# Warm-up matmuls on a constant: 26 of 48 columns in place of six of 512, at the head of a gated attention and feed-forward kernel

## The chip, the cores and the metric

The kernel runs on one core of a Trainium2 chip. The metric is the device time of one execution in microseconds (us); lower is better. The core has a matrix engine (PE, whose weight loads are recorded apart as PEld), a vector engine (DVE), a scalar engine (ACT), a general engine (POOL), and a queue engine (SP) that here only issues DMA transfers.

## The reference

One input x of 2048 tokens by 640 features feeds two branches, and a gate for each token mixes them.

```python
def _A_ref(x, wqkv, w_phi, wo):                      # 32 heads of 20
    q, k, v = split(x @ wqkv)
    pq = einsum("bhsd,hdf->bhsf", q, w_phi); pk = einsum("bhsd,hdf->bhsf", k, w_phi)
    phi_q = concat([softmax(pq), softmax(-pq)]); phi_k = concat([softmax(pk), softmax(-pk)])
    kv = einsum("bhsf,bhsd->bhfd", phi_k, v);  z = sum(phi_k, over s)
    o = einsum("bhqf,bhfd->bhqd", phi_q, kv) / (einsum("bhqf,bhf->bhq", phi_q, z) + 1e-6)
    return o @ wo
def _B_ref(x, w_gate, w_up, w_down):                 # F = 1728
    return (gelu(x @ w_gate) * (x @ w_up)) @ w_down
g = sigmoid((x * gate_w).sum(-1))
return g * _A_ref(x, ...) + (1 - g) * _B_ref(x, ...)
```

## The kernel before

Tokens are taken in 16 tiles of 128. Features lie on the 128 partitions in five chunks (`kt`), so a product of one token tile with a weight is five accumulating matmuls. The order of the work on each engine is written out by hand: each call of `sc.op` appends one instruction to one engine's program, with the semaphore waits that its reads and writes need. Between two instructions of PE no wait is put in. An engine works through its program strictly in that order.

The run has two stages. `attention_state` builds the transposed input `xT`, folds `w_phi` into the query and key weights (`fold`, L374), projects v, k and q for each token tile (`mm`, L396) and sums the attention state (`gram`, L506). `ffn` then does the gate and up projections in blocks of 512 tokens (`gateup`, again L396) and the down projections with the output projection (`down_pair`, L717), with the attention numerators (`num`, L662) in between.

The change touches the first instructions of PE. `attention_state` begins with matmuls whose two operands are a constant of ones (L543 to L545): each has a 128 by 128 stationary block and a moving block of `n` columns, and each writes to bank 0 of the accumulator `ps`, where the next thing written overwrites it. Nothing reads what they compute. The steps behind them, in PE's order, are these:

- `x_transpose(0)` and `x_transpose(1)` (L331): for each, ten PE transposes of 64 by 64 blocks. They need `xtok`, tokens that a DMA loads (L225, two transfers), and the identity that POOL makes. DVE and ACT copy the results to `xT` (L341, L339).
- six more matmuls on the constant (L551, 64 rows, 128 columns), then `x_transpose(2)` and `(3)`, which need the second `xtok` transfer.
- `v_step` (L408): for each of five chunks and four tiles, one matmul of 480 and one of 160 columns. They need `xT` and the weight chunk `w` (L245, five transfers).
- `gate_column` (L356), then `v_tile(4)` and `(5)` (L396), three folds (L374), and so on. `v_tile(6)` is the first that needs `xT` of tiles 6 and 7.

`xT` of the tiles from 4 on comes by transposing DMAs (L233), as do the transposed weights `wkT` and `wqT` (L229). SP issues all of these one after another: `xtok` twice, five chunks of `w`, `xT` of tiles 4 and 5, `wkT`, `xT` of tiles 6 and 7, `wqT`, and the rest of `xT`. None of them waits for PE.

Of the kernel before, what the change touches and what calls it, by code (L numbers as in the profile page):

```python
# [107 lines left out]
class _Kernel:  # L108
# [430 lines left out]
    def attention_state(self):  # L539
        NT = self.NT  # L540
        sc = self.sc
        ones = self.nc.const_aps.tensor(1.0, [P, 512], BF16)
        for n in (512, 512, 512, 512, 512, 512, 128, 128, 128):  # L543
            sc.op("pe", lambda e: e.matmul(self.bank(0, n), ones[:, 0:P], ones[:, 0:n], start=True, stop=True),
                  writes=[("ps", 0)])  # L545
        vs, ve, xt = self.v_step, self.v_first_evac, self.x_transpose
        xt(0, "d")
        xt(1, "a")
        for i in range(3):
            for a, b in ((0, 2), (64, 3)):  # L550
                sc.op("pe", lambda e: e.matmul(self.bank(b, P), ones[a:a + 64, 0:P], ones[a:a + 64, 0:P], start=True,  # L551
                                               stop=True), writes=[("ps", b)])
        xt(2, "d")
        xt(3, "a")
        for kt in range(4):
            for t in range(4):
                vs(t, kt)
        self.blockdiag()
        self.gate_column(6)
        for t in range(4):  # L560
            vs(t, 4)
            ve([t], "ad"[t % 2], False)
            if t == 2:
                ve([0, 1, 2], "a", True)
        ve([3], "d", True)
        f, v, k, q = self.fold, self.v_tile, self.k_tile, self.q_tile
        v(4, 6)
        v(5, 0)
        f(0, "k", (2, 3))
        f(1, "k", (4, 5))  # L570
        f(2, "k", (6, 7))
        self.strip(6)
        f(3, "k", (0, 1))
        self.strip(0)
        v(6, 2)
        f(4, "k", (4, 5))
        v(7, 6)
        k(0, 0)
        f(0, "q", (2, 3))
        f(1, "q", (4, 5))  # L580
        k(1, 6)
        f(2, "q", (2, 3))
        self.k_sums(0)
        k(2, 0)
        f(3, "q", (2, 3))
        self.strip(2)
        f(4, "q", (4, 5))
        self.k_scale(0)
        k(3, 6)
        v(8, 0)  # L590
        for t in range(1, 4):
            self.k_norm(t)
        nk, nv, ng = 4, 9, 0
        pieces = self.gate_pieces()
        for s in range(NT):
            r = s % 4
            if r != 1:
                k(nk, 2)
                self.k_norm(nk)
                nk += 1  # L600
            if s and r != 0:
                self.gram(ng)
                ng += 1
            if s and r in (0, 1):
                v(nv, 0)
                nv += 1
            q(s, 6)
            if s:
                pieces.pop(0)()
        for p in pieces:  # L610
            p()
        self.down_weights()
# [240 lines left out]
```

## Time and profile before

| | |
|---|---|
| median of 3 runs | 284.88 us |
| lowest, highest | 284.87, 287.49 us |
| the profiled execution | 284.86 us |
| span of the profile, first to last instruction | 283.5 us |
| around the span | 284.86 - 283.5 = 1.36 us |
| PE busy, matmuls | 280.3 us of the span, 2922 matmuls |
| DVE, ACT, POOL busy | 172.8, 104.8, 13.2 us |
| DMA moved | 24.11 MB |
| granted clock, mean of the run | 1.000 |

Times in the profile count from the start of the span. "Idle" is the time that an engine stood still before an instruction, with what ended it. Matmuls are pipelined: a matmul's record lasts from its start to a modelled end, so records overlap and a busy PE need not stream at its best rate. The spacing between the starts of successive matmuls, or of their weight loads, is the better measure of pace. PEq stands for PE's sequencer and SPq for SP's issuing of DMAs; "issue" marks time in which an engine waited for nothing that the profile shows.

### The profile page before, as it was taken

The numbers are of one execution on the slowest core, as the hardware profiler recorded it, in microseconds if no ns is written. First come the engines' busy times: TensorE is split into PE (matmuls) and PEld (weight loads), VectorE is DVE, ScalarE is ACT, GpSimd is POOL, SyncE is SP. The second block draws the span as 40 slices with busy tenths as digits, with TensorE's granted clock in tenths as the row PEclk, the third lists the DMA queues.
The fourth block names the chain that finished last, engine by engine and source line by source line (L and its number), as shares of the span: only waits on it lengthen the run. The fifth ranks groups of instructions, "written<-read, shape, count | busy, mean of one in ns | idle before, by whom it ended". The sixth has DMA issues, their size and how long they took to land.

```text
span 283.5 us, 6887 instructions
## 1 busy us (share of the span) xinstructions
PE 280.3 (99%) x2922; PEld 174.7 (62%) x2922; DVE 172.8 (61%) x325; ACT 104.8 (37%) x191; POOL 13.2 (5%) x67
## 2 busy tenths in 40 slices
PE   8999999999999999999999999999999999999996
PEld 5677777777754444444444444445777777777786
DVE  1369999999995332667242334325883883884801
ACT  4357888887852223222332223231112112012011
POOL 7500101110000000000000000000000000000000
DMA  8994398989999500011000000000133233232221
GB/s 227 189 219 91 60 198 179 192 180 165 171 250 353 146 0 0 2 23 24 2 0 0 0 2 0 0 0 2 25 50 85 58 44 76 72 44 76 73 73 49
DMA packets 58922, 24.11 MB, mean 85 GB/s; under 512 B 50954, under 2 KB 58378, under 8 KB 58890
## 3 DMA queue, kind: packets, MB, share of 16 engines
q1 hardware_dynamic: 58224, 23.63, 38.8%
q8 instruction: 23, 0.38, 0.6%
q10 hardware_dynamic: 666, 0.03, 0.2%
q14 instruction: 9, 0.07, 0.1%
HBM read 9.04 MB, written 2.62 MB: 41 GB/s over the span
## 4 chain that ended last, share of the span: by engine, by line
PE 94%; SPq 3%; DMA 2%; issue 0%; ACT 0%
PE ps L396 61%; PE ps L717 28%; PE ps L662 2%; DMA xT<-in_A_x_dram 2%; PE ps L506 2%; SPq L229 1%; SPq L245 1%; PE ps L374 1%; SPq L233 1%; SPq L225 0%; ACT outsb L730 0%
## 5 line engine op out<-in xcount | busy, mean ns | idle before, releaser
L396 PE MATMUL ps<-xT,wu_sb 128*128 128x512 bf16 x260 | 64.6, 379 | 0.0
L396 PE MATMUL ps<-xT,wg_sb 128*128 128x512 bf16 x260 | 64.6, 379 | 0.0
L633 ACT ACTIVATE gl<-ps 128x512 bf16<-128x512 f32 x52 | 31.1, 598 | 76.0 <-PE ps L396 73.8
L635 DVE TENSOR_TENSOR hT<-ps,gl 128x512 bf16<-128x512 f32 x39 | 26.7, 691 | 43.2 <-PE ps L396 43.2
L717 PE MATMUL ps<-wd_sb,hT 64*128 64x320 bf16 x648 | 48.4, 296 | 0.0
L396 PEld LDWEIGHTS ps<-xT,wu_sb 128*128 128x128 bf16 x260 | 25.4, 98 | 30.9 <-DVE hT L635 0.4
L396 PEld LDWEIGHTS ps<-xT,wg_sb 128*128 128x128 bf16 x260 | 25.0, 98 | 29.4
L730 ACT ACTIVATE outsb<-ps,Gm 128x320 bf16<-128x320 f32 (+2 forms) x31 | 14.6, 516 | 71.7 <-PE ps L717 71.7
L396 PE MATMUL ps<-w,xT 128*128 128x304 bf16 (+3 forms) x280 | 40.6, 296 | 0.3 <-DMA xT<-in_A_x_dram 0.3
L717 PEld LDWEIGHTS ps<-wd_sb,hT 64*128 64x128 bf16 x648 | 30.9, 94 | 12.2 <-issue 0.4
L396 PEld LDWEIGHTS ps<-w,xT 128*128 128x128 bf16 x280 | 26.4, 97 | 10.2 <-DMA xT<-in_A_x_dram 0.5
L717 PE MATMUL ps<-wo_sb,goT 64*128 64x320 bf16 (+2 forms) x340 | 26.5, 288 | 0.0
L495 DVE TENSOR_TENSOR Ek<-Ek,Dk 128x1320 bf16<-128x1320 bf16 x16 | 24.5, 1532 | 0.5
L688 DVE TENSOR_TENSOR O<-ps,RH 128x640 bf16<-128x640 f32 x32 | 24.8, 817 | 0.0
L486 DVE TENSOR_REDUCE Dk<-Ek 128x66 f32<-128x1320 bf16 x16 | 24.3, 1520 | 0.0
L396 PE MATMUL ps<-wq,xT 128*128 128x304 bf16 x160 | 23.3, 292 | 0.0
L453 ACT ACTIVATE Eqt<-ps 128x627 bf16<-128x627 f32 x32 | 20.5, 694 | 6.5 <-PE ps L396 6.5
L453 ACT ACTIVATE Ek<-ps 128x627 bf16<-128x627 f32 x32 | 20.5, 694 | 2.8 <-PE ps L396 2.6
L635 DVE TENSOR_TENSOR xT<-ps,gl 128x512 bf16<-128x512 f32 x13 | 9.0, 692 | 18.2 <-PE ps L396 18.2
L717 PEld LDWEIGHTS ps<-wo_sb,goT 64*128 64x128 bf16 x340 | 15.9, 94 | 5.3
L396 PEld LDWEIGHTS ps<-wq,xT 128*128 128x128 bf16 x160 | 15.0, 98 | 4.5
L717 PE MATMUL ps<-wd_sb,xT 64*128 64x320 bf16 (+2 forms) x270 | 16.0, 269 | 0.0
(77 smaller groups left out, 180.1 us busy)
## 6 DMA issues: line engine op xcount, KB each, us to landing
out_dram<-outsb SPq DMA_DIRECT2D x7, 320.0 KB, 2.3
wd_sb<-in_B_w_down_dram SPq DMA_DIRECT2D x1, 2080.0 KB, 10.6
wg_sb<-in_B_w_gate_dram SPq DMA_DIRECT2D x5, 224.0 KB, 4.0
wu_sb<-in_B_w_up_dram SPq DMA_DIRECT2D x5, 224.0 KB, 3.4
wg_sb<-in_B_w_gate_dram SPq DMA_DIRECT2D x5, 192.0 KB, 3.7
wu_sb<-in_B_w_up_dram SPq DMA_DIRECT2D x5, 192.0 KB, 3.3
w<-in_A_wqkv_dram SPq DMA_DIRECT2D x5, 160.0 KB, 4.0
wo_sb<-in_A_wo_dram SPq DMA_DIRECT2D x1, 800.0 KB, 9.6
```

The lines of the kernel that those rows point to most:

```text
L229: sc.dma("sp", lambda e: e.dma_start_transpose(T[:, :, :], self.wqkv[:, c0:c0 + D]), writes=[key])
L396: self.sc.op("pe", lambda e: e.matmul(self.ps[:, bank * 512 + c0:bank * 512 + c0 + n], lhs, rhs, start=first, stop=fin), reads=reads, writ ...
L453: self.sc.op("act", lambda e: e.activation(dst, src, AF.Exp, scale=scale), reads=[("ps", b), ("ps", b + 1)], writes=[(name, sl, s)])
L486: self.sc.op("dve", lambda e: e.tensor_reduce(self.Dk[:, se, 0, :].rearrange("p (u h) -> p u h", h=self.HG), self.k_view(se), AX.X, ALU.ad ...
L495: sc.op("dve", lambda e: e.tensor_tensor(v, v, R.rearrange("p (u h) -> p u h", h=self.HG).unsqueeze(3).to_broadcast([P, 2 * self.G, self.H ...
L506: self.sc.op("pe", lambda e: e.matmul(self.bank(b)[:, c:c + n], self.Ek[:, se, g * P:(g + 1) * P], va[:, w * g:w * g + n], start=(t == 0 a ...
L633: sc.op("act", lambda e: e.activation(self.gl[:, slot, :], self.bank(banks[0]), AF.Gelu_apprx_tanh), reads=[("ps", banks[0])], writes=[("g ...
L635: sc.op("dve", lambda e: e.tensor_tensor(hT, self.bank(banks[1]), self.gl[:, slot, :], ALU.mult), reads=[("ps", banks[1]), ("gl", slot)], ...
L662: sc.op("pe", lambda e: e.matmul(self.ps[:, o:o + n], self.Eq[a:a + 64, g, t * P:(t + 1) * P], self.KV[a:a + 64, g, 0:n], start=(g in (0, ...
L688: dve(lambda e, o=o, f=f, s=s: e.tensor_tensor(o, V[s][:, :, 0:DH], f, ALU.mult), rb + [key(6 + s)], [("O", s, sl)], guard=old)
L717: sc.op("pe", lambda e: e.matmul(self.bank(bk, w), lhs, rhs, start=opens and x == 0, stop=end and not opens, skip_group_check=True), reads ...
L730: sc.op("act", lambda e: e.activation(dst, self.bank(bk, w), AF.Copy, scale=g), reads=rd, writes=wr)
```

## The change

The list of column counts of the constant matmuls is replaced. Before, there are six of 512 columns and three of 128; after, 26 of 48 columns and the same three of 128.

```diff
         ones = self.nc.const_aps.tensor(1.0, [P, 512], BF16)
-        for n in (512, 512, 512, 512, 512, 512, 128, 128, 128):
+        for n in [48] * 26 + [128] * 3:
             sc.op("pe", lambda e: e.matmul(self.bank(0, n), ones[:, 0:P], ones[:, 0:n], start=True, stop=True),
                   writes=[("ps", 0)])
```

The columns streamed by this loop go from 6 x 512 + 3 x 128 = 3456 to 26 x 48 + 3 x 128 = 1632, and its matmuls, each with a weight load, from 9 to 29. All else in the program stays as it is and where it is.

## The prediction

> **What bounds the kernel now.** I read the busy times of the page first, then what PE waited for over the whole run, then the chain of waits that ends at 30 us, and last the first 6 us of PE instruction by instruction.
>
> ```profile
> PE 280.3 (99%) x2922; PEld 174.7 (62%) x2922; DVE 172.8 (61%) x325; ACT 104.8 (37%) x191; POOL 13.2 (5%) x67
> ```
> ```profile
> PE ps L544 <- PEq L838: 0.8, 1, 0.8
> PE ps L396 <- DMA xT<-in_A_x_dram: 0.3, 1, 0.3
> ```
>
> The second fence is the whole answer for PE as the waiting engine. After its start at 0.84 us, PE stands still once in the run, for 0.3 us, and a DMA ends that. From there to the end PE alone sets the time, so whatever delays it past that wait is paid in full at the end. What paces the part ahead of it is in the chain that leads into that wait:
>
> ```profile
> 4.09 1.93 SPq L233
> 6.02 0.05 issue
> 6.07 3.70 SPq L229
> 9.77 0.04 issue
> 9.81 5.65 DMA xT<-in_A_x_dram
> 15.46 0.05 issue
> 15.51 1.54 PE ps L396 x10
> ```
>
> The columns are start, length and what. SP's issues follow one another and end in the transposing DMA for tiles 6 and 7, which lands at 15.46 us. Nothing of PE stands in this chain. Ahead of 15.5 us PE therefore has a slack, and these two rows give its size (the number in brackets is the idle time before the row):
>
> ```profile
> 15.51 0.76 PE L396 MATMUL ps<-w,xT 128*128 128x345 bf16 x4 [0.27 <-DMA xT<-in_A_x_dram]
> ```
> ```profile
> 15.51 0.56 PEld L396 LDWEIGHTS ps<-w,xT 128*128 128x128 bf16 x5 [0.46 <-DMA xT<-in_A_x_dram]
> ```
>
> The slack is 0.27 us by the matmul's modelled end and 0.46 us by the weight load. Matmul records overlap (the 512-column ones last 0.63 us and start 0.43 us apart), so a modelled end understates the idle time, and I take a value near the upper one, 0.40 us.
>
> Now the start, first as PE's weight loads in order of time:
>
> ```profile
> 1.22 0.15 PEld L544 LDWEIGHTS ps<-const-bfloat16-1.0 128*128 128x128 bf16 x1 [0.27 <-issue]
> 1.65 0.15 PEld L544 LDWEIGHTS ps<-const-bfloat16-1.0 128*128 128x128 bf16 x1 [0.28 <-issue]
> 2.07 0.15 PEld L544 LDWEIGHTS ps<-const-bfloat16-1.0 128*128 128x128 bf16 x1 [0.28 <-issue]
> ...
> 3.35 0.25 PEld L544 LDWEIGHTS ps<-const-bfloat16-1.0 128*128 128x128 bf16 x2 [0.28 <-issue]
> 3.80 0.19 PEld L331 LDWEIGHTS ps<-ident,xtok 64*128 64x128 bf16 x6 [0.20 <-DMA xtok<-in_A_x_dram]
> ```
>
> Two things are to be seen. The 512-column matmuls start 0.43 us apart, while a window of 5 us in the gate and up stage (100 to 105 us) holds 25 of the same width, some 0.21 us each: PE starts at half its later pace. And the transposes at 3.80 us are released by the landing of `xtok`, not by the end of the warm-up. Where the pace doubles shows in the groups of two stretches, 4 to 6 us and 6 to 9 us, where the last number is the mean record in ns:
>
> ```profile
> L408 PE MATMUL ps<-w,xT 128*128 128x480 bf16 x2 | 0.8, 456 | 0.0
> ```
> ```profile
> L408 PE MATMUL ps<-w,xT 128*128 128x480 bf16 x12 | 3.4, 364 | 0.0
> ```
>
> Two matmuls of 480 columns start between 4 and 6 us, at a mean of 456 ns; from 6 us on each takes 364. So one of the two took 2 x 456 - 364 = 548 ns, and that is the first (it starts at 5.31). The pace changes inside it: I put the change at 5.7 us, which is 5.7 - 0.84 = 4.86 us after PE's first matmul. The granted clock of the profile reads 1.00 in every stretch, so this doubling has to be read from the pace. PE was kept at work nearly without a break over those 4.86 us.
>
> **The warm-up itself.** Removed are six matmuls of 0.43 us (the first 0.38), from 0.84 to 3.35 us: 2.51 us. Added are 26 of 48 columns with 26 weight loads. At the slow pace 512 columns take 0.43 us, so 48 take 0.040 us, together 1.04 us. The nearest row for such short matmuls with a full weight load each is `gram`: 11 matmuls of 63 columns in 0.34 us of the chain at 29.52 us, 0.031 us each at the fast pace, so at most 0.062 us if everything in it is halved, together 1.61 us. I take the lower one, because the three 128-column matmuls in the same loop are paced by their columns (the load of 0.15 us lies beside them). With the three at 0.107 us (0.32 us), which stay, the loop ends at 2.2 us, at the latest at 2.8. On the path this is worth nothing: the transposes still wait for `xtok` until 3.80. A gain is excluded altogether, since a PE that came earlier to 15.5 us would wait there for the `xT` that lands at 15.46. The 20 further matmuls and 20 loads add no wait of another engine, since nothing reads bank 0 until the transposes overwrite it, and SP's queue is not touched. New is a standstill of PE from 2.2 (2.8) to 3.80: 1.6 us (1.0 us).
>
> **The pace afterwards.** This is the term that decides, and the trace holds no row with a break in the warm-up, so I bound it. From below: the doubling stays at 5.7 us, price nothing, and a price below nothing is excluded by the wait at 15.46. From above: the doubling needs 4.86 us of full streaming, and neither the broken start nor the small transposes count; the 480-column matmuls begin at 5.31, so it comes at 10.2 us. In between: the count starts anew after the standstill, at 3.80, and the doubling comes at 3.80 + 4.86 = 8.66 us. I take this one, since it is nearest to what the rows show, 4.86 us of work with breaks of no more than 0.2 us. From 5.7 to 8.66 us PE then does half of what it did: (8.66 - 5.70) / 2 = 1.48 us lost. The upper bound gives (10.2 - 5.7) / 2 = 2.25 us.
>
> The row, then, is a doubling 4.86 us after the first matmul. The Trainium skill ("TensorE: Matmul & The Clock Gate", Part 1, the HAM clock gate) states that the gate opens after a busy free-running window of some 3.4 us, and that the budget is time at work, not a number of matmuls; that speaks against many short ones in place of few long ones. By this rule the doubling would move by one whole window, to 5.7 + 3.4 = 9.1 us, an estimate that costs 1.7 us instead of 1.48. The same page (Part 4) says that transposes don't count as busy in the same way, which would make the window that ends at 5.7 emptier still; no row here shows it.
>
> **The sum.** The profiled execution took 284.86 us, and the median of the runs is 284.88, so it needs no correction. 284.86 + 0 (warm-up) + 1.48 (later doubling) - 0.40 (slack at 15.5 us, which the delay fills first) = 285.94, so 285.9 us. By the skill's window it would be 284.86 + 1.7 - 0.4 = 286.2.
>
> What comes late with PE costs nothing more: DVE, ACT and POOL then have longer for the `xT` copies, `BD` and the constants, and the loads of `w` land for a PE that comes later. After 15.5 us the order of all engines is the same, shifted by 1.1 us, up to the last store.
>
> **The rivals.**
>
> - *The doubling stays where it is* (the end on the other side: not slower). It needs 1.0 to 1.6 us less work than there was. For it: the pace also held through the breaks at 3.7 and 5.2 us, so it doesn't ask for work without any break. Against it: the new standstill is five times longer than any break there. It decides as long as the doubling comes before 5.7 + 2 x 0.40 = 6.5 us, since the slack covers that: 284.9 us.
> - *The doubling is later still.* With full streaming only from 5.31 us: 284.86 + 2.25 - 0.40 = 286.7 us. One of the three timed runs of before stands at 287.49, 2.6 us above the others; if a missed doubling made that run, it came at 5.7 + 2 x (2.6 + 0.4) = 11.7 us, and the change could make this the usual case: 287.5, with a step more 288. Nothing in the profile shows what made that run.
> - *The warm-up does not get shorter.* If each weight load of 0.147 us must run before its matmul, a pair takes 0.19 us, 26 take 4.9 us, and the loop ends at 6.0 us, 2.2 us after `xtok`. The work that stood between 3.8 and 5.7 us (1.9 us) then runs at the fast pace in 0.95 us, so 2.2 + 0.95 - 1.9 = 1.25 us are lost, and 0.85 us remain after the slack: 285.7. Against it: `gram` shows full loads hidden at 0.031 us a pair.
>
> **How the numbers follow.** Chances: doubling unmoved 0.24 (284.7 to 285.1), forecast with a restart or one step 0.56 (285.3 to 286.7), later still 0.14 (286.7 to 288.2), loads in the way 0.04 (285.4 to 286.0), something that I don't see, on the fast side, 0.02. The range goes from 284.7 to 287.0 and leaves out most of the late case and the last one, some 0.14. The forecast's own range is 285.3 to 286.7. One per cent of 284.88 is 2.85 us, about what a measurement of this kernel can tell from no change; faster by that is below 282.0, excluded by the `xT` landing, 0.02. Slower by that is above 287.7, the upper part of the late case, 0.09. The rest, 0.89, is within 1%: my forecast is a loss of 0.4%.
>
> **What would show it.** The 48-column weight loads should start 0.04 us apart (0.06 at most; 0.15 or more means the third rival). PEld should stand idle for 1.0 to 1.6 us before the transposes, ended by the `xtok` DMA at 3.8 us. In the stretches of 4 to 6 and 6 to 9 us the 480-column records should be long (about 550 to 600 ns) until some 8.7 us and 364 after. The idle time at 15.5 us on the `xT` DMA should be gone, with the first matmul of `v_tile(6)` about 1.1 us later. If the records turn short before 6.5 us, the first rival holds. I would be wrong in kind if PE waited anew after 16 us, or if the transfers landed at other times.

## The result, and the profile after

| | before | after |
|---|---|---|
| median of 22 runs | 285.0 us | 286.25 us |
| lowest to highest | 284.52 to 287.49 us | 285.58 to 287.28 us |
| the profiled execution, its span | 284.86, 283.5 us | 286.63, 285.3 us |

The ratio is 1.0041, with a 95% interval of 1.0031 to 1.0051: the change costs 1.25 us of the median, against 1.1 us forecast, and the time lies inside the forecast's own range. The profiled execution of after lies above its median; its distance to the one of before is 286.63 - 284.86 = 1.77 us.

The page's busy times and PE's waits over the whole run, after:

```profile
PE 279.8 (98%) x2929; PEld 175.7 (62%) x2942; DVE 172.7 (61%) x325; ACT 104.7 (37%) x191; POOL 13.2 (5%) x67
```
```profile
PE ps L331 <- DMA xtok<-in_A_x_dram: 1.5, 1, 1.5
PE ps L544 <- PEq L838: 0.8, 1, 0.8
PE ps L396 <- DVE w L386: 0.3, 1, 0.3
PE ps L396 <- issue: 0.2, 1, 0.2
```

The busy times of DVE, ACT and POOL have not moved by more than 0.1 us. PE has a standstill of 1.5 us ahead of the transposes (L331), as forecast, and one of 0.3 us that was not forecast: an L396 matmul waits for DVE at L386, the read-out of a fold. (The last row, 0.2 us with nothing waited for, stands at 128.7 us, far behind the change.) The start, as PE's weight loads in order of time:

```profile
0.81 1.28 PEld L544 LDWEIGHTS ps<-const-bfloat16-1.0 128*128 128x128 bf16 x29 [0.81 <-issue]
3.81 0.56 PEld L331 LDWEIGHTS ps<-ident,xtok 64*128 64x128 bf16 x20 [1.72 <-DMA xtok<-in_A_x_dram]
```

All 29 loads fit into 1.28 us and are over by 2.1 us; the transposes start at 3.81 us as before, when `xtok` lands. Where the pace doubles shows in the group of the 480-column matmuls from 5 to 13 us, all 20 of them, before and then after:

```profile
L408 PE MATMUL ps<-w,xT 128*128 128x480 bf16 x20 | 5.8, 373 | 0.0
```
```profile
L408 PE MATMUL ps<-w,xT 128*128 128x480 bf16 x20 | 7.6, 457 | 0.0
```

From 6 to 9 us the same group tells what one takes at the first, halved pace:

```profile
L408 PE MATMUL ps<-w,xT 128*128 128x480 bf16 x6 | 3.3, 607 | 0.0
```

At the halved pace one takes 607 ns, at the full pace 364 (the row of 6 to 9 us before). The mean over 20 therefore counts those at half pace: 20 x (373 - 364) / (607 - 364) = 0.74 before, 20 x (457 - 364) / 243 = 7.65 after. Each of the 20 goes with one of 160 columns, and 640 columns take 0.53 us at half pace (512 take 0.43) and half of that at full pace. So the doubling stands at 5.31 + 0.74 x 0.53 = 5.7 us before and at 5.32 + 7.65 x 0.53 = 9.4 us after, and 6.9 more pairs at half pace cost 6.9 x 0.267 = 1.84 us. The span grew by 1.8. One term holds the whole loss. What became of the slack that was to take 0.40 us from it is shown by the chain of waits, after:

```profile
16.35 0.81 DVE w L386
17.16 0.14 issue
17.29 1.53 PE ps L396 x10
```

The 17.29 row is `v_tile(6)`, the one that waited for `xT` before. It begins 0.14 us after DVE has read out the fold f(0), whose banks it overwrites. The transposing DMA of its `xT` was issued later than in the kernel before, at 11.44 us, and landed 5.5 us after that, at 16.9, 0.2 us ahead of the end of DVE's read-out. Now DVE's rows in order of time, in the kernel before:

```profile
14.32 0.19 DVE L385 COPY wref<-ps 128x32 f32<-128x32 f32 x1 [2.27 <-PE ps L374]
14.55 2.19 DVE L386 TENSOR_TENSOR w<-ps,wref 128x608 bf16<-128x608 f32 x3
```

The first of the three L386 instructions (2.19 / 3, and 0.8 alone) ends at 15.35, and `v_tile(6)` began at 15.51, 0.16 us later. So in the kernel before two waits ended at the same point, the landing of `xT` at 15.46 and DVE's read-out. The second one moves with PE, since f(0) is PE's own work, and it leaves no slack.

### The profile page after: what moved, and what is told of

Same layout as the page of the kernel before. It is cut to its first block, busy times and chain, and to the rows that moved or that the text cites. A ratio compares the mean times of both kernels' runs of the same rounds, so it can differ in the third digit from the quotient of the medians.

```text
span 285.3 us, 6914 instructions
## 1 busy us (share of the span) xinstructions
PE 279.8 (98%) x2929; PEld 175.7 (62%) x2942; DVE 172.7 (61%) x325; ACT 104.7 (37%) x191; POOL 13.2 (5%) x67
## 4 chain that ended last, share of the span: by engine, by line
PE 97%; DMA 1%; issue 0%; DVE 0%; ACT 0%; DVEq 0%
PE ps L396 61%; PE ps L717 28%; PE ps L408 3%; PE ps L662 2%; PE ps L506 2%; DMA xtok<-in_A_x_dram 1%; PE ps L374 1%; PE ps L331 0%; DVE w L386 0%; ACT outsb L730 0%; PE ps L551 0%; DVE wref L385 0%; PE ps L356 0%; DVEq L42 0%
## 5 line engine op out<-in xcount | busy, mean ns | idle before, releaser
L396 PE MATMUL ps<-xT,wu_sb 128*128 128x512 bf16 x255 | 63.5, 379 | 0.2
L396 PE MATMUL ps<-xT,wg_sb 128*128 128x512 bf16 x252 | 63.0, 379 | 0.6 <-issue 0.2
L396 PEld LDWEIGHTS ps<-xT,wu_sb 128*128 128x128 bf16 x260 | 25.4, 98 | 30.8 <-DVE hT L635 0.4
L396 PEld LDWEIGHTS ps<-xT,wg_sb 128*128 128x128 bf16 x260 | 25.0, 98 | 29.4
L396 PE MATMUL ps<-w,xT 128*128 128x304 bf16 (+3 forms) x280 | 40.6, 295 | 0.3 <-DVE w L386 0.3
L396 PEld LDWEIGHTS ps<-w,xT 128*128 128x128 bf16 x280 | 26.4, 97 | 10.2 <-DMA xT<-in_A_x_dram 0.4
L396 PE MATMUL ps<-wq,xT 128*128 128x304 bf16 x160 | 23.2, 292 | 0.0
L396 PEld LDWEIGHTS ps<-wq,xT 128*128 128x128 bf16 x160 | 15.0, 97 | 4.5
```

Of the source, the lines that this page charges most:

```text
L396: self.sc.op("pe", lambda e: e.matmul(self.ps[:, bank * 512 + c0:bank * 512 + c0 + n], lhs, rhs, start=first, stop=fin), reads=reads, writ ...
```

## The experiments

In each table row, "at half pace" is the number of 480-column matmuls in the profile that ran at half pace, worked out as above, and the doubling follows from it. The kernels came in three groups, each beside its own runs of before (medians 284.97, 285.14 and 285.06 us).

| kernel | median us | ratio to before (95%) | at half pace | doubling at us | profiled us |
|---|---|---|---|---|---|
| before | 285.0 | 1 | 0.74 | 5.7 | 284.86 |
| after | 286.25 | 1.0041 (1.0031 to 1.0051) | 7.65 | 9.4 | 286.63 |
| e1_64_short | 285.16 | 1.0006 (0.9993 to 1.0019) | 0 | ahead of 4.2 | 284.88 |
| e2_none | 285.94 | 1.0034 (1.0016 to 1.0052) | 3.3 | 7.0 | 285.62 |
| e3_late | 285.73 | 1.0020 (1.0011 to 1.0029) | 4.3 | 7.6 | 285.73 |
| e5_few_long | 286.04 | 1.0035 (1.0021 to 1.0049) | 5.3 | 8.1 | 286.00 |

### Length or number: e1_64_short and e5_few_long

```diff
-        for n in [48] * 26 + [128] * 3:
+        for n in [48] * 64 + [128] * 3:                  # e1_64_short
+        for n in (512, 512, 224, 128, 128, 128):         # e5_few_long
```

> The warm-up is 64 matmuls of 48 columns and the three of 128: 64 x 0.040 = 2.56 us, as long as the six of 512 were, with as many columns, but with 38 more matmuls than the change. Theory (what counts is how long PE is kept at work without a break before 3.8 us): the pace doubles where it did in the kernel before, some time from 4.3 to 7.7 us, and the time is that of before, 285.0 us, ratio 1.000. Rival (short matmuls with a weight load each do not count as work, or cost something by their number): as slow as the change or slower, 286.2 us or more, ratio 1.004, with the doubling after 7.2 us.

> The warm-up is six matmuls of 512, 512, 224, 128, 128 and 128 columns: 1632 columns, as many as with the change and as long (1.36 us), but in 6 matmuls and not 29. Theory (what counts is how long PE is kept at work): as the change, 286.2 us, ratio to before 1.004, a standstill from 2.2 to 3.8 us, the doubling between 7 and 10.5 us. Rival (the number of short matmuls with their weight loads is what costs): as before, 285.0 us, ratio 1.000.

Both went as the theory had it, but for the doubling of e1_64_short, which came a little ahead of the 4.3 us that the theory gave as the earliest. With 67 short matmuls in place of nine long ones and no change in length, the time is that of before; with six matmuls in place of 29 and the length of the change, it is that of the change. PE's rows in order of time show the first of them, e1_64_short:

```profile
0.84 3.04 PE L544 MATMUL ps<-const-bfloat16-1.0 128*128 128x48 bf16 x67 [0.84 <-PEq L838]
3.81 0.52 PE L331 MATMUL ps<-ident,xtok 64*128 64x64 bf16 x20
```

67 matmuls fill the same 3.04 us that nine did. The 20 transposes take 0.52 us where they took 0.72 before: the pace doubled inside them, some 1.5 us or more earlier than in the profile of before, whose warm-up has the same length. Yet this execution, at 284.88 us, was no faster than 284.86. PE's waits of the same kernel say why:

```profile
PE ps L408 <- DMA w<-in_A_wqkv_dram: 0.6, 1, 0.6
PE ps L396 <- DVE w L386: 0.2, 1, 0.2
```

PE came early to the first v step and waited 0.6 us there for the weights. An earlier doubling brings nothing in this kernel; only a later one costs.

### What the short warm-up is worth, and where: e2_none and e3_late

```diff
-        for n in [48] * 26 + [128] * 3:
+        for n in []:                                     # e2_none
-                  writes=[("ps", 0)])
+                  reads=[("mask", 0)], writes=[("ps", 0)])   # e3_late, with the 26 and 3 of the change
```

> The loop of constant matmuls is left out altogether, so PE's first work is the transposes at 3.8 us. Theory (the work has to be unbroken, so the 1.3 us of the change, which end at 2.2 us, are lost in the standstill of 1.6 us behind them): as the change, 286.2 us, ratio to before 1.004, doubling between 7.2 and 10.6 us. Rival (a sum of work since the start counts): the doubling comes 1.3 us later than with the change, so 0.65 us more, 286.9 us, ratio 1.0066. If the transposes count for nothing, as the Trainium skill's clock-gate page suggests in Part 4, the doubling cannot come before 5.3 + 3.4 = 8.7 us, an estimate, and the time is above 286.3 in every run.

> The 26 of 48 columns and the three of 128 are the same, but they wait for a tile that POOL writes until about 2.3 us, so that they end at about 3.7 us and the standstill lies ahead of them and not behind. Theory (unbroken work): the stretch of work begins at 2.3 us and not at 3.8, so the doubling comes 1.5 us earlier than with the change on average, between 5.8 and 9.1 us, worth 0.7 us: 285.5 us, ratio 1.002. Rival (sum of work, or number of columns): no different from the change, 286.2 us, ratio 1.004.

Without any warm-up the time is as with the change (the intervals of the two ratios overlap, and 285.94 is below 286.25): the 1.3 us of work that end at 2.1 us are worth nothing. Its doubling, at 7.0 us, came just ahead of the 7.2 expected. A sum of work is ruled out, since it asked for 286.9. The same 29 matmuls, made to lie directly ahead of the transposes, cost 0.76 us against the kernel before where the change costs 1.25: 285.73, against 285.5 expected and 286.2 by the rival. Against no warm-up at all they save 0.21 us, and there the two intervals overlap, so that this last gain is not clear. PE's weight loads of e3_late in order of time:

```profile
2.30 1.27 PEld L544 LDWEIGHTS ps<-const-bfloat16-1.0 128*128 128x128 bf16 x29 [2.30 <-POOL mask L258]
3.77 0.56 PEld L331 LDWEIGHTS ps<-ident,xtok 64*128 64x128 bf16 x20 [0.20 <-DMA xtok<-in_A_x_dram]
```

It is the same work of 1.27 us, with the standstill now ahead of it and 0.2 us behind it. The order of the work is otherwise that of the change.

The 480-column groups from 5 to 13 us give each profile's doubling, for e2_none, e3_late and e5_few_long in turn:

```profile
L408 PE MATMUL ps<-w,xT 128*128 128x480 bf16 x20 | 6.5, 404 | 0.0
```
```profile
L408 PE MATMUL ps<-w,xT 128*128 128x480 bf16 x20 | 6.7, 416 | 0.0
```
```profile
L408 PE MATMUL ps<-w,xT 128*128 128x480 bf16 x20 | 7.0, 429 | 0.0
```

The more of them ran at half pace, the longer the execution. At 0.267 us for each beyond the 0.74 of before they ask for 0.7, 0.9, 1.2 and, after, 1.8 us; the profiled times stand 0.76, 0.87, 1.14 and 1.77 us above before's. Each agrees within 0.1 us, with no slack of 0.40 us in it.

### The slack at `v_tile(6)`: e8_delay

```diff
+        for i in range(4):
+            sc.op("pe", lambda e: e.matmul(self.bank(7), ones[:, 0:P], ones[:, :], start=True, stop=True),
+                  writes=[("ps", 7)])
         self.blockdiag()
         self.gate_column(6)
```

> The kernel before, with four more matmuls of 512 columns on the constant behind the first sixteen v steps, into a bank that is free there: at the fast pace they take 4 x 0.216 = 0.86 us and delay all of PE's later work ahead of 15.5 us. Theory (there is no slack at v_tile(6), since the wait there is for DVE's read-out of f(0), which moves with PE): the whole delay arrives, 285.0 + 0.86 = 285.9 us, ratio 1.003, and the break of 0.42 us in front of v_tile(6) stays as long as it was. Rival (the prediction's slack of 0.40 us is filled first): 285.0 + 0.46 = 285.5 us, ratio 1.0016, and the break is gone.

Measured were 285.89 us, ratio 1.0030 (1.0020 to 1.0039), against 285.06 us: 0.83 of the 0.86 us arrived. By the interval it is 0.57 to 1.11 us, and the rival's 0.46 lies outside. The wait stayed. PE's rows in order of time, e8_delay:

```profile
14.87 1.50 PE L374 MATMUL ps<-BD,wkT 128*128 128x140 bf16 x24
16.61 1.53 PE L396 MATMUL ps<-w,xT 128*128 128x345 bf16 x10 [0.25 <-DVE w L386]
```

`v_tile(6)` comes 1.1 us later than in the kernel before, and PE still stands idle ahead of it, 0.25 us by the modelled end, now for DVE. It cannot be `xT`, whose transfer was issued at 9.74 us and landed 5.3 us later, at 15.0:

```profile
9.74 1.58 SPq L233 DMA_TRANSPOSE xT<-in_A_x_dram  x1
DMA to landing us min/median/max: 5.3/5.3/5.3
```

The 1.1 us are the 0.86 of the four matmuls and some 0.2 from before them, where PE waited 0.44 us for `xtok` at 5.2 us; and the profiled execution is 285.94 - 284.86 = 1.08 us longer than that of before. The same bracket with the same 0.25 stands in after, e2_none, e3_late and e5_few_long. There was no slack to fill.

### Other orders at `v_tile(6)`: e4_fold_first, e6_banks_after, e7_banks_before

e4_fold_first moves f(0) ahead of `v_tile(5)` in the changed kernel; e6_banks_after also exchanges the banks of f(3) and `v_tile(6)`; e7_banks_before does the same in the kernel before.

```diff
-        v(5, 0)
+        self.strip(0)                # e6, e7
         f(0, "k", (2, 3))
+        v(5, 0)
         f(1, "k", (4, 5))
         f(2, "k", (6, 7))
         self.strip(6)
-        f(3, "k", (0, 1))
-        self.strip(0)
-        v(6, 2)
+        f(3, "k", (2, 3))            # e6, e7; e4 keeps these three as they were
+        v(6, 0)
```

> The changed kernel with the first key fold, f(0), moved ahead of v_tile(5), so that DVE has read its banks out before v_tile(6) needs them. Theory (in the changed kernel the slack of 0.40 us at v_tile(6) was not filled, since a wait for DVE's read-out of f(0) stood just behind the wait for xT and took its place): the wait on DVE at L386 of 0.3 us before v_tile(6) is gone, and v_tile(6) starts up to 0.4 us earlier where xT has landed by then: 285.9 us, ratio to before 1.003. Rival (the slack was filled as predicted and the whole loss is the later doubling): no change from the changed kernel, 286.2 us, ratio 1.004.

> The changed kernel with f(0) ahead of v_tile(5), f(3) in banks 2 and 3 and v_tile(6) in banks 0 and 1, so that v_tile(6) waits for ACT's read-out of v_tile(5) and not for DVE's of f(0), with nothing else of the order changed. Theory (the slack of 0.40 us was never there, since the wait for DVE at v_tile(6) lies just behind the wait for xT): the wait at L386 is gone, v_tile(6) follows f(3) without a break where xT has landed, and the time is up to 0.4 us below the change: 285.9 us, ratio to before 1.003. Rival (xT's landing or another read-out takes its place): 286.2 us, ratio 1.004, with a wait of the same length on something else.

> The kernel before with the same order and banks as e6_banks_after. Theory (at v_tile(6) the waits for xT and for DVE end within 0.1 us of one another in the kernel before): with DVE's wait out of the way, xT's landing still holds PE in most executions: 284.9 us, ratio 1.000, and PE waits for the DMA of xT alone. Rival (DVE's wait was what held PE): v_tile(6) starts 0.4 us earlier, 284.6 us, ratio 0.9986.

None of the three gained what was hoped for, and e7_banks_before lost 0.9 us, which neither its theory (284.9) nor its rival (284.6) had. Measured were 286.42 (ratio 1.0046, 1.0032 to 1.0060), 286.29 (1.0038, 1.0023 to 1.0053) and 286.06 us (1.0033, 1.0015 to 1.0050). In each the wait at L386 is gone, and PE's waits show what stands in its place, in e4_fold_first, e6_banks_after and e7_banks_before:

```profile
PE ps L374 <- ACT gcol L443: 0.2, 1, 0.2
```
```profile
PE ps L374 <- DMA wkT<-in_A_wqkv_dram: 0.3, 1, 0.3
```
```profile
PE ps L374 <- DMA wkT<-in_A_wqkv_dram: 1.2, 1, 1.2
```

In e4_fold_first a fold waits for ACT's read-out of `v_tile(5)`; in the other two f(0), now earlier, waits for `wkT`. The times of e4_fold_first and e6_banks_after lie where their rivals put them (286.2). As another wait took the place of the one removed, these runs do not decide about the slack, for which e8_delay stands; they show that the loads and read-outs around 14 to 16 us leave no free place for 0.4 us in these orders. No version was found that beats the kernel before.

## Why the prediction was right, point by point

**The warm-up itself.** Right. 48-column matmuls follow one another at 0.040 us (29 loads in 1.28 us, and the 38 more of e1_64_short in 1.52 us more), the value taken; the standstill is 1.72 us by the weight loads, against 1.6. The transposes did not move, so the earlier end of the warm-up is worth nothing on the path. The third rival, loads in the way, fell with this.

**The pace afterwards.** The mechanism was right and is shown, not only argued: e1_64_short and e5_few_long set aside number and shape, e2_none the sum of work, and e3_late moves the time by moving the same work. Mis-sized, for the profiled execution, is the term: I put the doubling at 8.66 us, 1.48 us of loss, and the profile has 9.4 and 1.84. The row that I took (4.86 us of work) is no constant: the doubling came 4.9 us after the first matmul in before and, with the same length of warm-up, about 3 to 3.4 us after it in e1_64_short.

The Trainium skill ("TensorE: Matmul & The Clock Gate", Part 1, the HAM clock gate) says that the gate looks at a free-running window of some 3.4 us. That the place varies with nothing changed ahead of it, the profiles show. With the start of the change the doubling came at 9.4 us (after), 8.9 (e4_fold_first, where the 20 matmuls of 480 columns average 448 ns) and 8.4 (e6_banks_after, 436 ns). With the start of before it came at 5.7 us (before), between 4.6 and 5.2 (e8_delay) and inside the first transposes, at about 4.1 (e7_banks_before, where their 20 weight loads took 0.38 us against 0.56). The length of the window is not shown. The 3.7 us between before and after are one draw from each; the 22 runs of after spread over 287.28 - 285.58 = 1.70 us, half of 3.4, but the 12 of e2_none spread over 1.90.

The same page's Part 4 says that transposes do not count as busy in the same way. Read so that they count for nothing, as in the expectation of e2_none, it does not hold here: the first work of that kernel is the transposes at 3.76 us, and in the profiled execution, the fastest of its 12, the doubling came at 7.0, 3.3 us later and not at 8.7 or behind. Without the transposes there were only the six matmuls on the constant and 1.7 us of work, from 5.3 us. How much the transposes count, and how full a window must be, no run here shows.

**The slack.** This step failed: "- 0.40 (slack at 15.5 us, which the delay fills first)". The profile named the DMA as what ended the wait, and I took the idle time as free. DVE's read-out of f(0) ended 0.1 us before that landing and moves with PE, so a delay of PE is not taken up. e8_delay has 0.83 of 0.86 us arriving. Left out of the sum, the slack takes the forecast from 285.94 to 286.34 us, and the median is 286.25.

**The sum.** In the profiled executions it is 284.86 + 1.84 - 0.07 = 286.63, where the 0.07 us is what remains unexplained. Against the forecast loss of 1.08 us both errors point the same way there: the doubling's term was 0.36 us too small and the slack of 0.40 left only 0.07, which makes the 0.69 us that 1.77 lies above 1.08. That the median came so close, 1.25 us, is in part luck, since the profiled execution of after lies 0.38 us above its median: the median, 286.25, is 1.39 us above the profiled before, which by half of the delay is a doubling near 5.7 + 2 x 1.39 = 8.5 us, an estimate, and there the 1.48 us were about right. The doubling of a median execution was not profiled. In the kernel before an early one gains nothing (e1_64_short: PE waits 0.6 us for `w`).

**The rivals.** The doubling did not stay (an unmoved one would give 285.0), and it was not later still in the usual case: 18 of the 22 runs lie below the 286.7 us of that rival. "I would be wrong in kind if PE waited anew after 16 us": it does, for 0.25 us, but the same standstill was there before under another name. The other sign, "if the transfers landed at other times", came true as well: `xT` of tiles 6 and 7 landed at 16.9 us and not at 15.46, since SP's issue of `wkT` took longer. It came about when PE was done with what stood before (16.85 us by the weight loads, 17.04 by the modelled end), so it took little of the slack; what held PE to 17.29 was DVE's read-out, as in e8_delay, where `xT` landed at 15.0. What made the run of before at 287.49 us, and another of before at 287.31 beside the experiments, stays open: no profile fell on such a run.

## What to carry to other kernels

Here a warm-up was worth the time for which it kept the matrix engine at work up to the moment when real work began; work followed by a standstill of 1.7 us was worth as little as none (e2_none). So size it by the landing of the first input, whatever the number and width of its matmuls. If it must be short, late is better than early (e3_late, 285.73 against 286.25), though against none at all (285.94) the gain is not clear. And before an idle stretch is counted as slack, see whether a second wait ends close behind the one that the profile names, and whether that one moves with the delay.

## What the runs showed of the hardware

- The profile's granted clock read 1.00 in every profiled execution, also where PE kept half pace until 9.4 us (after): the halving has to be read from the spacing of starts or from the records (607 against 364 ns for 480 columns).
- Transposes follow the same pace: the weight loads of 20 of 64 by 64 blocks took 0.56 us at half pace and 0.35 us at full pace (the first and the second 20 of e8_delay; by the matmul records 0.71 and 0.47).
- A break need not reset everything: in before, breaks of 0.2 us ahead of the transposes and 0.1 us ahead of the first v step (5.3 us) did not keep the doubling from coming at 5.7 us, and in e8_delay it came by 5.2 us although PE's weight loads stood still from 4.6 to 5.2 us. Once the pace had doubled, a standstill of 1.2 us did not undo it (e7_banks_before, ahead of f(0): the 140-column matmuls behind it last 225 ns, as in before). How long a break ahead of the doubling may be was not tried between 0.6 and 1.6 us.
- The issue of the transposing DMAs varies between executions with the same start: SP's issue of `wkT` took 3.70 us in before (the chain shown with the prediction), 4.29 in e7_banks_before and 3.46 in e8_delay. In after it took 5.10 us, from 6.30 to 11.40 us, which puts all the transfers behind it later too, and 5.14 and 5.17 us in e4_fold_first and e6_banks_after, which begin like it. Whether the change itself lengthens it stays open.
